# K and V laid out with 32 adjacent keys of one batch per partition (8 KB rows) in a fused attention and feed-forward gradient kernel

## Chip, cores, metric

One core of one Trainium2 chip. The metric is device time in microseconds (us); a quoted time is the median of a kernel's executions. Executions carry a state: "fast" or "slow" (over 1.5% above the fastest of the same kernel). All ratios below use fast executions alone. In the profile's lines PE is TensorE, PEld its weight loads, DVE VectorE, ACT ScalarE and POOL GpSimd.

## The reference, cut to what matters

The kernel computes the output and all eight gradients of one decode step: layer norm, then attention over the last 1024 keys of a cache (B = 4 batches, 8 key-value heads, 4 query heads for each, head size 128, one query), and beside it a gated feed-forward (512 to 1792).

```python
W = min(4096, max(256, Sk // 4))                  # 1024 of Sk = 4096 keys
k = jnp.repeat(k_cache[:, :, Sk - W:, :], rep, axis=1)
v = jnp.repeat(v_cache[:, :, Sk - W:, :], rep, axis=1)
scores = jnp.einsum("bhqd,bhkd->bhqk", q, k) * (Dh ** -0.5)
p = _softmax(scores, axis=-1)
o = jnp.einsum("bhqk,bhkd->bhqd", p, v)           # ... @ wo
# out = x + A(xn) + B(xn); then the gradients of x, K, V, wq, wo and the three B weights
```

Of the 112 MB that the kernel moves, 50 MB are zeros: the gradients of the 3072 keys of each head that the query does not see, written by DMA from one zero tile. K and V come in with 16.8 MB, and dK and dV of the 1024 keys in use go out with 16.8 MB.

## The kernel before, the parts that matter

The kernel runs four rounds of two key-value heads (`GP = 2`). In each it loads K and V, transposes them on TensorE for the scores, takes the softmax, transposes P (and dS) for the products o and dq, and makes dV and dK by outer products. Small pieces of output work lie in a list `bg` and are set in between other work by `tick`. The helper `evac` copies a result of TensorE out of its accumulation memory (PSUM), on VectorE or ScalarE. All DMA goes through three queues: loads from SyncE (q1), zeros from ScalarE (q10), stores from GpSimd (q0).

```python
outp = ctx.enter_context(tc.tile_pool(name="outp", bufs=3))      # buffers of output pieces (osb_*)
...
def load_kv(t, k, g):                   # partition m: 8 adjacent keys of each of 4 batches, 2 KB runs
    tl = kvpool[...].tile([P, B, J, Dh], BF16, name=nm, tag=nm)
    nc.sync.dma_start(out=tl[:].rearrange("p b j d -> p b (j d)"),
                  in_=src[:, t * GP + g, K0:Sk, :].rearrange("b (m j) d -> m b (j d)", j=J))
...
def scores(t, k):                       # for each head g and batch b
    for j in range(J):
        nc.tensor.transpose(T_ps[:, j, :], blks[(t, g)][:, b, j, :], ident[:])
    evac(T_sb[:], T_ps[:].rearrange("p j m -> p (j m)"), 1024, half=True)
    for q in range(NQ):                 # a quarter of the keys in each column tile
        nc.tensor.matmul(ps[q * RG:(q + 1) * RG, :], lhsT=lf[:, s * RG:(s + 1) * RG],
                         rhs=T_sb[:, q * WQ:(q + 1) * WQ], ..., tile_position=(0, q * RG))
    tick(2)
...
def by_quarter(src, nm):                # spread for dV and dK, on GpSimd
    nc.gpsimd.tensor_tensor(out=dst[:], in0=src[:]..., in1=qmsk[:]..., op=ALU.mult)

def transposed(src, nm):                # 2 transposes of P or dS itself, not of its spread
    for jj in range(JQ):
        nc.tensor.transpose(pT_ps[:, jj, :], src[:, jj * P:(jj + 1) * P], ident[:])
    evac(pT[:], pT_ps[:], 256, half=True)

def odq(t, k):                          # four batches in four column tiles, side by side
    for g in range(GP):
        for j in range(J):
            for b in range(B):
                nc.tensor.matmul(od_ps[b * RB:b * RB + rep, k, g, :], lhsT=pT[:, jj, c0:c0 + rep],
                                 rhs=blks[(t, g)][:, b, j, :], ..., tile_position=(0, b * RB))
...
# a round: masks, scores(K), softmax + dvdk(V), scores(V), softmax_d + dvdk(K), odq(o),
#          pre(t + 1), odq(dq), fin, load_next, dw
```

## Time and profile before

| before | |
|---|---|
| time, median of the first 3 executions | 289.91 us |
| span of the profiled execution | 287.5 us |
| DMA engines busy | 99.1% of the span: 284.9 us, idle 2.6 us |
| TensorE (PE) busy | 206.9 us |
| waits for stores of `osb_o`, in the chain | 17.92, 19.11 and 4.22 us |

The prediction shows the page's own lines. Three more lines of before are needed later. They are from the groups by shape; after the shapes come count, busy us, mean ns of one, then the idle us of the engine before them and what ended it:

```profile
L341 PE MATMUL S_ps<-T_sb,dom 128*32 128x256 bf16 x128 | 10.5, 310 | 5.1 <-DVE T_sb L94 5.1
...
L361 PE MATMUL pT_ps<-ident,P_b 128*128 128x128 bf16 x8 | 1.5, 283 | 3.5 <-ACT P_b L389 3.5
L361 PE MATMUL pT_ps<-ident,dS_b 128*128 128x128 bf16 x8 | 1.3, 244 | 4.9 <-DVE dS_b L405 4.9
```

The eight transposes of P and the eight of dS cost 2.8 us, and PE stands before them for 8.4 us, because P and dS come straight from ScalarE and VectorE. And from the waits (engine, tile, line, releaser; sum, count, longest), the two engines that fill the output buffers wait 37.0 us for a store to free one:

```profile
ACT osb_q L92 <- DMA out_dram<-osb_o: 20.1, 3, 9.5
...
DVE osb_q L94 <- DMA out_dram<-osb_o: 16.9, 3, 7.1
```

### The profile page before, as it was taken

The page shows a single profiled execution, that of the slowest core. Times are in us where ns is not written, and L with a number is a line of the kernel's source. Part 1 is how long each engine was busy: PE and PEld are TensorE (multiplying, and loading weights), DVE is VectorE, ACT ScalarE, POOL GpSimd, SP SyncE. Part 2 cuts the span into 40 slices and gives each one's busy share as a digit, 9 for nine tenths or more (in the row PEclk, how much of TensorE's full clock was granted, in tenths as well). Part 3 has the DMA queues.
Part 4 walks back from the last instruction along what each step waited for, and adds up shares of the span by engine and source line. Part 5 has one row for each costly group of instructions (what it writes and reads, how often), then busy time and mean ns, then how long its engine had stood idle before and what let it go on. Part 6 is the DMA issues. An engine that isn't in the chain of part 4 may idle for free.

```text
span 287.5 us, 6821 instructions
## 1 busy us (share of the span) xinstructions
PE 206.9 (72%) x2956; PEld 141.5 (49%) x2956; DVE 144.9 (50%) x310; ACT 113.7 (40%) x217; POOL 66.7 (23%) x84
## 2 busy tenths in 40 slices
PE   1397994983977999545689996546998679597710
PEld 0386882652644765333357654323665355364310
DVE  5484572333564567312626674126476525537770
ACT  1201653443442467312424563134355444336610
POOL 7000130441303152311033323110252132112410
PEclk9996899597897899795958898959799969959975
DMA  5999999999999999999998999999999999999897
GB/s 138 381 389 376 385 399 421 413 403 429 423 426 427 413 372 401 435 415 427 416 419 330 327 363 429 426 427 411 415 413 380 395 390 412 406 415 360 337 393 295
DMA packets 30182, 112.38 MB, mean 391 GB/s; under 512 B 1537, under 2 KB 7689, under 8 KB 26057
## 3 DMA queue, kind: packets, MB, share of 16 engines
q10 hardware_dynamic: 4612, 50.46, 41.9%
q1 hardware_dynamic: 17732, 30.81, 29.4%
q0 software_dynamic: 7808, 30.67, 27.3%
q8 instruction: 23, 0.38, 0.5%
q14 instruction: 7, 0.05, 0.0%
HBM read 30.93 MB, written 81.01 MB: 389 GB/s over the span
## 4 chain that ended last, share of the span: by engine, by line
PE 47%; DMA 28%; DVE 14%; issue 4%; ACT 2%; POOL 1%; SPq 0%; DVEq 0%; ACTq 0%; POOLq 0%
DMA out_dram<-osb_o 14%; PE T_ps L336 9%; PE kv_ps L444 7%; DMA out_dram<-stg_dv 4%; DVE T_sb L94 4%; PE S_ps L341 4%; DMA wd_sb<-in_B_w_down_dram 4%; DMA out_dram<-osb_d 3%; PE od_ps L416 3%; PE woT_ps L288 3%; PE wqT_ps L508 3%; DMA out_dram<-osb_g 2%; PE acc_ps L181 2%; PE wgT_ps L648 2%; PE wdT_ps L536 2%
## 5 line engine op out<-in xcount | busy, mean ns | idle before, releaser
L94 DVE COPY T_sb<-T_ps 128x1024 bf16<-128x1024 bf16 x64 | 44.2, 691 | 34.2 <-PE T_ps L336 33.7
L92 ACT CAST stg_dv<-kv_ps 128x512 bf16<-128x512 f32 x52 | 28.8, 589 | 43.2 <-PE kv_ps L444 42.8
L92 ACT CAST stg_dk<-kv_ps 128x512 bf16<-128x512 f32 x46 | 25.0, 588 | 15.4 <-PE kv_ps L444 13.1
L336 PE MATMUL T_ps<-ident,vb 128*128 128x128 bf16 x256 | 26.1, 251 | 6.6 <-DVE osb_q L94 6.6
L336 PEld LDWEIGHTS <-vb 128*128 128x128 bf16 x256 | 20.0, 114 | 12.7 <-issue 8.9
L92 ACT CAST osb_q<-dwq_ps 128x512 bf16<-128x512 f32 x25 | 13.6, 589 | 30.4 <-DMA out_dram<-osb_o 20.1
L336 PE MATMUL T_ps<-ident,kb 128*128 128x128 bf16 x256 | 24.4, 228 | 0.5 <-ACT stg_dk L92 0.3
L336 PEld LDWEIGHTS <-kb 128*128 128x128 bf16 x256 | 18.1, 101 | 12.4 <-issue 5.0
L444 PE MATMUL kv_ps<-domr,P_q 128*128 128x512 bf16 x64 | 23.9, 435 | 0.0
L444 PE MATMUL kv_ps<-qmr,dS_q 128*128 128x512 bf16 x64 | 20.9, 410 | 1.5 <-ACT stg_dk L92 1.0
L92 ACT CAST osb_g<-dwg_ps 128x384 bf16<-128x384 f32 (+1 forms) x30 | 14.5, 534 | 17.6 <-PE dwg_ps L621 8.1
L94 DVE COPY woT<-woT_ps 128x1024 bf16<-128x1024 bf16 x16 | 11.1, 692 | 17.2 <-PE woT_ps L288 17.2
L478 PE MATMUL dwq_ps<-od_r,xnm 128*128 128x256 bf16 x64 | 12.5, 320 | 6.8 <-DVE osb_q L94 6.6
L352 POOL TENSOR_TENSOR dS_q<-dS_b,qmsk 128x1024 bf16<-128x1024 bf16 x4 | 7.5, 1884 | 34.3 <-DVE dS_b L405 34.3
L92 ACT CAST osb_o<-dwo_ps 128x512 bf16<-128x512 f32 x23 | 12.7, 588 | 7.0 <-PE dwo_ps L463 6.8
L341 PE MATMUL S_ps<-T_sb,dom 128*32 128x256 bf16 x128 | 10.5, 310 | 5.1 <-DVE T_sb L94 5.1
L98 POOL DMA_DIRECT2D out_dram<-osb_q x8 | 5.8, 731 | 34.6 <-ACT osb_q L92 34.6
L94 DVE COPY wqT<-wqT_ps 128x1024 bf16<-128x1024 bf16 x16 | 11.0, 687 | 5.5 <-PE wqT_ps L508 5.3
L508 PEld LDWEIGHTS <-wq_sb 128*128 128x128 bf16 x128 | 11.1, 120 | 5.3 <-issue 4.3
L94 DVE CAST osb_q<-dwq_ps 128x512 bf16<-128x512 f32 x7 | 4.7, 689 | 16.9 <-DMA out_dram<-osb_o 16.9
L98 POOL DMA_DIRECT2D out_dram<-stg_dv x8 | 6.2, 774 | 30.4 <-ACT stg_dv L92 30.4
L94 DVE CAST stg_dk<-kv_ps 128x512 bf16<-128x512 f32 x18 | 12.0, 685 | 2.4 <-PE kv_ps L444 1.2
(187 smaller groups left out, 381.1 us busy)
## 6 DMA issues: line engine op xcount, KB each, us to landing
out_dram<-ztile ACTq DMA_DIRECT2D x8, 3072.0 KB, 16.5
out_dram<-ztile ACTq DMA_DIRECT2D x16, 1536.0 KB, 15.3
kb<-in_A_k_cache_dram SPq DMA_DIRECT2D x8, 1024.0 KB, 17.1
vb<-in_A_v_cache_dram SPq DMA_DIRECT2D x8, 1024.0 KB, 49.5
out_dram<-stg_dv POOLq DMA_DIRECT2D x8, 1024.0 KB, 10.1
out_dram<-stg_dk POOLq DMA_DIRECT2D x8, 1024.0 KB, 8.4
wo_sb<-in_A_wo_dram SPq DMA_DIRECT2D x4, 1024.0 KB, 10.2
wq_sb<-in_A_wq_dram SPq DMA_DIRECT2D x4, 1024.0 KB, 14.2
```

Source lines behind the costliest of these rows:

```text
L92: last.append(nc.scalar.copy(out=out, in_=in_))
L94: return nc.vector.tensor_copy(out=out, in_=in_)
L98: d = eng.dma_start(out=out, in_=in_)
L181: nc.tensor.matmul(ps[:, c, :], lhsT=lf(c), rhs=rhs, start=(k == 0), stop=(k == len(terms) - 1))
L288: nc.tensor.transpose(wT_ps[:, i, c, :], wo_sb[:, 2 * h2 + i, c * P:(c + 1) * P], ident[:])
L336: nc.tensor.transpose(T_ps[:, j, :], blks[(t, g)][:, b, j, :], ident[:])
L341: nc.tensor.matmul(ps[q * RG:(q + 1) * RG, :], lhsT=lf[:, s * RG:(s + 1) * RG], rhs=T_sb[:, q * WQ:(q + 1) * WQ], start=(g == 0 and b == 0 ...
L352: nc.gpsimd.tensor_tensor(out=dst[:], in0=src[:].unsqueeze(1).broadcast_to([P, NQ, WQ]), in1=qmsk[:].unsqueeze(2).broadcast_to([P, NQ, WQ] ...
L416: nc.tensor.matmul(od_ps[b * RB:b * RB + rep, k, g, :], lhsT=pT[:, jj, c0:c0 + rep], rhs=blks[(t, g)][:, b, j, :], start=(j == 0), stop=(j ...
L444: nc.tensor.matmul(mps[:].rearrange("p b d -> p (b d)"), lhsT=src[:, q, jj * P:(jj + 1) * P], rhs=mr[:, g].rearrange("p b d -> p (b d)"), ...
L478: nc.tensor.matmul(mps[:, i].rearrange("p g d -> p (g d)"), lhsT=xnm[:, i2 * 2 + i, c * P:(c + 1) * P], rhs=dq_r[:].rearrange("p g d -> p ...
L508: nc.tensor.transpose(wT_ps[:, i, c, :], wq_sb[:, c, h * Dh:(h + 1) * Dh], ident[:])
```

## The change

Intent: one partition holds 32 adjacent keys of one batch, so K and V come, and dK and dV go, in 8 KB runs instead of 2 and 4 KB, with fewer packets. The price is in the compute. A transposed block now has the four batches interleaved (key block and batch share the partition index), so the scores read T_sb with a step of 4. P and dS must be spread by batch *before* they are transposed. The o and dq products go over all four batches at once, in one column tile.

```diff
 def load_kv(t, k, g):
-    tl = ....tile([P, B, J, Dh], ...)          # J = 8
-    nc.sync.dma_start(out=tl[:].rearrange("p b j d -> p b (j d)"),
+    tl = ....tile([P, J, Dh], ...)             # J = 32; partition = (key block m, batch b)
+    nc.sync.dma_start(out=tl[:].rearrange("p j d -> p (j d)"),
 def scores(t, k):
-                    nc.tensor.matmul(ps[q * RG:(q + 1) * RG, :], lhsT=lf[:, s * RG:(s + 1) * RG],
-                                     rhs=T_sb[:, q * WQ:(q + 1) * WQ], ...
+                    nc.tensor.matmul(ps[b * RG:(b + 1) * RG, :], lhsT=lf[:, b, s * RG:(s + 1) * RG],
+                                     rhs=T_sb[:, :, b], ...
-    def by_quarter(src, nm):
+    def by_batch(src, nm):
+        nc.gpsimd.tensor_tensor(out=dst[:].rearrange("p j (m b) -> p (j m) b", b=B),
+                                in0=src[:].unsqueeze(2).broadcast_to([P, WQ, B]),
+                                in1=bmsk[:].unsqueeze(1).broadcast_to([P, WQ, B]), op=ALU.mult)
 def transposed(src, nm):                        # JQ = 8 transposes, was 2
-        evac(pT[:], pT_ps[:], 256, half=True)
+        evac(pT[:].rearrange("p j (h b) -> p j b h", b=B), pT_ps[:].rearrange("p j (b h) -> p j b h", b=B), 1024, ...)
 def softmax(t):
-        st[t].update(E=E_f, rr=rr, PT=transposed(P_b, "PT"), P=by_quarter(P_b, "P_q"))
+        P_x = by_batch(P_b, "P_x")
+        st[t].update(E=E_f, rr=rr, PT=transposed(P_x, "PT"), P=P_x)
 def odq(t, k):
-                for b in range(B):
-                    nc.tensor.matmul(od_ps[b * RB:b * RB + rep, k, g, :], lhsT=pT[:, jj, c0:c0 + rep],
-                                     rhs=blks[(t, g)][:, b, j, :], ..., tile_position=(0, b * RB))
+                nc.tensor.matmul(od_ps[0:rep * B, k, g, :], lhsT=pT[:, j % JQ, j // JQ, g], rhs=blks[(t, g)][:, j, :], ...)
 ...                                             # stores of dV and dK in 8 KB runs; masks; FFN rows: cut
```

> **What bounds the kernel now.** I read the page first, then the DMA view in short windows, the windows view by stage, the chain of waits, and last the groups by shape and the timeline. The page (busy time by engine, DMA share in 40 slices, DMA queues with packets, MB and share of 16 engines' span):
>
> ```profile
> PE 206.9 (72%) x2956; PEld 141.5 (49%) x2956; DVE 144.9 (50%) x310; ACT 113.7 (40%) x217; POOL 66.7 (23%) x84
> ...
> DMA  5999999999999999999998999999999999999897
> ...
> q10 hardware_dynamic: 4612, 50.46, 41.9%
> q1 hardware_dynamic: 17732, 30.81, 29.4%
> q0 software_dynamic: 7808, 30.67, 27.3%
> ```
>
> The DMA digits are 9 nearly everywhere, and the three queues add to 98.6% of the span (99.1% with instruction fetch): the DMA engines have no spare time. PE at 72% has some. So bytes per busy microsecond matter first. A queue's rate while busy is its MB over its share times 287.5 us: q10 (the zeros) 50.46/(0.419 x 287.5) = 419 GB/s, q0 (stores) 391 GB/s, q1 (loads) 364 GB/s. q1 mixes weights with K and V; from 24 to 32 us it carries K and V alone:
>
> ```profile
> q1 hardware_dynamic: 1535, 3.05, 103.4%
> ```
>
> That is 2 KB packets at 3.05/(1.034 x 8) = 369 GB/s. The stretch 206 to 214 us has all three queues at work:
>
> ```profile
> q10 hardware_dynamic: 197, 2.10, 62.4%
> q0 software_dynamic: 191, 0.78, 23.9%
> q1 hardware_dynamic: 205, 0.41, 13.3%
> ```
>
> About 200 packets each: the queues take turns packet by packet, so a queue's share follows its packet size (12 KB, 4 KB, 2 KB). Next, stages (stretch, its us, busy us of PE, PEld, DVE, ACT and POOL with counts, granted clock, DMA share, GB/s):
>
> ```profile
> 132.00:164.00 32.00, 27.76 (x429) 18.66 (x429) 16.25 (x36) 13.32 (x26) 8.63 (x7) 0.78 0.99 383
> ...
> 171.00:190.00 19.00, 9.64 (x129) 6.51 (x127) 5.63 (x13) 4.54 (x11) 3.87 (x4) 0.84 1.03 424
> 190.00:217.00 27.00, 22.65 (x363) 15.41 (x363) 15.37 (x34) 12.45 (x24) 8.07 (x7) 0.86 1.02 416
> ...
> 264.00:276.00 12.00, 7.10 (x38) 3.54 (x36) 7.98 (x13) 7.12 (x13) 3.76 (x5) 1.00 0.92 339
> 276.00:287.50 11.50, 0.30 (x3) 0.00 (x0) 3.90 (x9) 0.00 (x0) 0.72 (x1) 0.50 0.84 344
> ```
>
> PE is busy 27.8 of 32 us between 132 and 164 and 22.7 of 27 us between 190 and 217, but half idle from 171 to 190. The chain says why (start, us, what):
>
> ```profile
> 113.48 17.92 DMA out_dram<-osb_o
> ...
> 170.73 19.11 DMA out_dram<-osb_o
> ...
> 252.06 12.71 DMA out_dram<-stg_dv
> ```
>
> At the end of rounds 0 and 1 of the four rounds (t = 0..3), compute waits some 18 us for a store to free an output buffer. In between it is PE that paces, and only the work already queued keeps the DMA busy. Bytes issued minus bytes landed, in us at 400 GB/s, give that reserve: about 5 us at 104, 2.3 us at 160, 2.0 us at 216, 2.5 us at 236, under 1 us at 268. These low points are where added compute would leave the DMA idle.
>
> **What the Trainium skill says.** (1) "DMA: Bandwidth & Descriptors", Why small descriptors are slow: a fixed overhead of some cycles per packet, besides descriptor bytes. The trace agrees in direction: 369 GB/s at 2 KB, 419 at 12 KB. (2) "TensorE: Matmul & The Clock Gate", Part 3 (Packing small matmuls): matmuls at different column tiles run at once. The trace agrees, see od_ps below. (3) "Advanced Engine Details and Errata", VectorE Performance Modes: two elements a cycle from 16-bit data need a unit step innermost. The 1024-element copy in 691 ns fits two a cycle; no stepped copy stands in this trace. (4) The same page, Memory Cachelines: SBUF reads need two hits per 16-byte line for full speed; a step of 4 bf16 just has two. No run yet shows it.
>
> **The change, part by part.**
>
> DMA loads. 16 loads of 1.05 MB go from 2 KB to 8 KB packets. The trace's mean load packet takes 51 ns at 1 KB, 87 at 2 KB, 146 at 3.5 KB, so some 38 ns per further KB: estimate 323 ns at 8 KB, 406 GB/s. 16.8 MB take 45.5 us at 369 and 41.3 at 406: minus 4.2 us.
>
> DMA stores. 16 stores of 1.05 MB have 4 KB packets now (168 ns mean; two rows each); 7 KB packets take 273 ns and 12 KB ones 468, so 8 KB would take about 312 ns, 420 GB/s: minus 3 us. The means include crowded stretches (medians give half of it); I count 5.5 us for both, about 1.9%.
>
> Turns. K and V loads then move 8 KB a turn against 2, their stores 8 against 4, the zeros still 12. Zeros thus last longer as a reserve, and stg stores land sooner: worth about 1 us at each of the big waits.
>
> Compute, from the groups and the timeline:
>
> ```profile
> L94 DVE COPY T_sb<-T_ps 128x1024 bf16<-128x1024 bf16 x64 | 44.2, 691 | 34.2 <-PE T_ps L336 33.7
> ...
> L352 POOL TENSOR_TENSOR P_q<-P_b,qmsk 128x1024 bf16<-128x1024 bf16 x4 | 7.5, 1887 | 9.2 <-ACT P_b L389 9.2
> ...
> L416 PE MATMUL od_ps<-vb,PT 128*4 128x128 bf16 x256 | 7.0, 238 | 0.0
> ...
> L94 DVE COPY PT<-pT_ps 128x256 bf16<-128x256 bf16 x4 | 1.2, 292 | 4.3 <-PE pT_ps L361 4.3
> ```
>
> ```profile
> 216.35 0.61 PE L336 MATMUL T_ps<-ident,kb 128*128 128x128 bf16 x8
> ...
> 251.06 1.06 PE L416 MATMUL od_ps<-kb,dST 128*4 128x128 bf16 x64
> ```
>
> The o and dq products (od_ps): 64 matmuls took 1.06 us, less one drain of 0.22 about 13 ns each, because four batches sit in four column tiles. The 8 transposes, one after another in the whole array, took 56 ns each. After the change the four batches share one product over all 128 partitions: still 64 matmuls (32 key blocks, 2 heads), now in one tile. 64 x 56 = 3.6 us, plus 2.7 us a time, 8 times: plus 21 us of PE, more where the clock is low. This is the largest cost.
>
> P and dS. The spread on GpSimd (1.89 us, size unchanged) now stands before the transposes: 8 transposes for 2 (plus 6 x 0.056 = 0.34 us PE) and an evacuation of 1024 elements with a stepped output for 292 ns. At one element a cycle[...] that is about 1.2 us, plus 0.9 us DVE. The latency grows by 1.9 + 0.3 + 0.9 = 3.1 us, 8 times. For P it lies beside the V scores; for dS beside the next round's weight products, but in round 3 nothing is left to hide it.
>
> Unchanged: T_sb copies, kv_ps products and their evacuations (8 pieces per head before and after), masks, dw. Removed: 36 of 48 small matmuls in the FFN rows, some mask set-up, store descriptors on GpSimd. All early or off the path: about 0.
>
> **The sum.** Round 0: about 5 us more PE, reserve 5 us: 0 to 1 us of DMA idle. Round 1, from 132 to 160: what is left of the V product (42 of 64) +1.8, the K product +2.7, transposes and copy +0.5, about 5; PE gaps take 1, the reserve 2.3: 2 us idle. Round 2: +3.5 less 2.0, and a faster DMA empties its reserve sooner: 2 us. Round 3: two products +5.4, dS +3.1, less about 4 us of waits for stores in the last stretch and under 1 us of reserve: 4 us. Sum about plus 8.5; minus 5.5 for the DMA: plus 3. 289.9 + 3.1 = **293.0 us**.
>
> **Rivals.** (a) The compute is hidden and the DMA gain shows whole: 284 us. For it: 98.6% DMA share and 18 us waits; against it: the low reserves after those waits. (b) Compute takes over: PE, in order, stands at the transposes until GpSimd has spread P or dS, about 2 us eight times, besides the longer products: 298 to 304 us. Against it: the timeline shows od_ps and other work moved between the score steps, so other matmuls can be set in there. (c) The score products read with a step of 4: if that halved their rate, some 0.2 us for each of 64 groups, 10 us or more of PE: over 300. (d) Larger packets of loads delay osb_o stores (still 4 KB a turn) and lengthen the 18 us waits; their bytes are the same, so I give it 1 us at most.
>
> **Range and chances.** Low end: (a) at 284. High end: (b), 303. Faster by over 2% (under 284.1) needs nearly all the DMA gain and no idle: 0.13. Slower by over 2% (over 295.7) needs about 3 us more than my sum, easy for round 3 or the transposes: 0.35. Within: 0.52.
>
> **What would show it.** K/V loads alone at 400 GB/s or more in the DMA view, about 8 KB per packet; od_ps 64 at a time in 3.6 us; PT copies near 1.2 us; T_sb and S_ps unchanged; DMA digits below 9 near the ends of rounds and after 236 us. If the DMA share stays at 99%, the time must fall and I am wrong on idle; if pT_ps shows PE waits of 2 us, rival (b). What would make the prediction wrong: a schedule that fills PE better than I think, or a slower spread on GpSimd with inner runs of 4.

## The result

| | before | after |
|---|---|---|
| median | 290.73 us (4 executions) | 334.86 us (4) |
| range | 289.87 to 291.81 | 332.85 to 337.37 |
| ratio of fast executions | | 1.152, 95% interval 1.142 to 1.162 |

A ratio is the mean time of one kernel's fast executions over that of the other's of the same rounds, so it is not quite the ratio of the medians. The change made the kernel 15% slower.

The profile after, the page (busy by engine, DMA share in 40 slices, the three queues with packets, MB and share):

```profile
PE 241.3 (72%) x2968; PEld 170.5 (51%) x2968; DVE 160.8 (48%) x310; ACT 115.6 (34%) x219; POOL 62.8 (19%) x77
...
DMA  7999999996993399999916999999339959971895
...
q10 hardware_dynamic: 4624, 50.46, 35.8%
q1 hardware_dynamic: 11600, 30.81, 24.5%
q0 software_dynamic: 5760, 30.67, 23.2%
```

Read the DMA digits first. A solid row of 9s before; now holes, which the windows view places at about 100 to 120, 168 to 180, 236 to 252 and 296 to 316 us, with smaller ones at 80 and 272 us. The first large one (stretch, its us, busy us of PE, PEld, DVE, ACT and POOL with counts, granted clock, DMA share, GB/s) shows PE at work nearly throughout while the DMA engines are busy for 41% of it:

```profile
100.00:120.00 20.00, 18.49 (x256) 14.33 (x256) 10.33 (x19) 7.01 (x14) 4.68 (x4) 0.78 0.41 152
```

The queues add to 83.5%, 83.9% with instruction fetch. Of a span of 335.7 us that is 281.7 us busy and 54.0 idle, against 284.9 and 2.6 before. So the DMA did get shorter, by 3.2 us, and all of the loss is DMA idleness: compute had become the bound. What of compute? The groups by shape:

```profile
L418 PE MATMUL od_ps<-kb,dST 128*16 128x128 bf16 x256 | 19.6, 245 | 0.0
L418 PE MATMUL od_ps<-vb,PT 128*16 128x128 bf16 x256 | 16.6, 219 | 0.0
L341 PE MATMUL S_ps<-T_sb,dom 128*32 128x256 bf16 x128 | 12.9, 388 | 3.4 <-DVE T_sb L96 3.4
...
L96 DVE COPY PT<-pT_ps 128x1024 bf16<-128x1024 bf16 x4 | 9.7, 2432 | 14.9 <-PE pT_ps L363 14.9
L96 DVE COPY dST<-pT_ps 128x1024 bf16<-128x1024 bf16 x4 | 9.7, 2423 | 12.4 <-PE pT_ps L363 12.4
L352 POOL TENSOR_TENSOR P_x<-P_b,bmsk 128x1024 bf16<-128x1024 bf16 x4 | 7.6, 1889 | 11.3 <-ACT P_b L392 11.3
...
L363 PE MATMUL pT_ps<-ident,P_x 128*128 128x128 bf16 x32 | 4.1, 311 | 11.4 <-POOL P_x L352 11.4
L363 PE MATMUL pT_ps<-ident,dS_x 128*128 128x128 bf16 x32 | 3.9, 296 | 13.0 <-POOL dS_x L352 13.0
```

Four things stand here. The od products take 36.2 us of PE against 13.7. The stepped copies of PT and dST take 2.43 us each against 0.29, 19.4 us in all. PE stands 24.4 us before the transposes, waiting for GpSimd, against 8.4. And the score products take 388 ns instead of 310 (for the K half 386 instead of 287). The end of the chain of waits shows the first three in a row (start us, length us, what), in the last round:

```profile
290.72 1.89 POOL dS_x L352
292.66 1.05 PE pT_ps L363 x8
293.74 2.43 DVE dST L96
296.58 5.27 PE od_ps L418 x64
```

The same stretch before: 0.29 us for the two transposes, 0.29 for the copy and 1.06 us for 64 od products. The granted clock makes it worse. In the timeline the eight transposes take 1.03 us after 3.31 us in which PE was idle, where the prediction's line of before has eight in 0.61 us. In round 2, at a granted clock of 1.00, 54 products take 3.11 us (213.58 us), so 64 would take about 3.7; in this last round they take 5.27, and the granted clock is 0.50 from 289.6 to 299.8 us. The Trainium skill ("TensorE: Matmul & The Clock Gate", Part 1) says that the clock falls to half after an idle window of about 3.4 us. The trace agrees that the low clock stands at PE's pauses, but here no wholly idle window came first: in the 3.4 us before 289.6 us PE was busy for 2.26 us at a granted clock of 1.00.

The clock is no rival for the whole loss. Over a fast execution its mean was 0.814 to 0.822 in the changed kernel and 0.825 to 0.852 before, but the run a_tiled below, at 0.796 to 0.821, was 17.5 us faster than the changed kernel.

### The profile page after: what moved, and what is told of

Its sections match the earlier page's. It is cut to its first block, busy times and chain, and to the rows that moved or that the text cites. A ratio compares the mean times of both kernels' runs of the same rounds, so it can differ in the third digit from the quotient of the medians.

```text
span 335.7 us, 6838 instructions
## 1 busy us (share of the span) xinstructions
PE 241.3 (72%) x2968; PEld 170.5 (51%) x2968; DVE 160.8 (48%) x310; ACT 115.6 (34%) x219; POOL 62.8 (19%) x77
## 5 line engine op out<-in xcount | busy, mean ns | idle before, releaser
L94 ACT CAST stg_dk<-kv_ps 128x512 bf16<-128x512 f32 x46 | 25.5, 588 | 16.2 <-PE kv_ps L444 13.6
L444 PE MATMUL kv_ps<-domr,P_x 128*128 128x512 bf16 x64 | 22.5, 409 | 1.0 <-DVE od_T L429 1.0
L94 ACT CAST osb_g<-dwg_ps 128x512 bf16<-128x512 f32 (+1 forms) x30 | 14.8, 535 | 23.9 <-PE dwg_ps L620 13.1
L444 PE MATMUL kv_ps<-qmr,dS_x 128*128 128x512 bf16 x64 | 21.4, 411 | 0.6 <-ACT stg_dv L94 0.2
L418 PE MATMUL od_ps<-kb,dST 128*16 128x128 bf16 x256 | 19.6, 245 | 0.0
L418 PEld LDWEIGHTS <-dST 128*16 128x16 bf16 x256 | 17.4, 102 | 2.0 <-issue 1.9
L96 DVE COPY PT<-pT_ps 128x1024 bf16<-128x1024 bf16 x4 | 9.7, 2432 | 14.9 <-PE pT_ps L363 14.9
L418 PE MATMUL od_ps<-vb,PT 128*16 128x128 bf16 x256 | 16.6, 219 | 0.0
L96 DVE COPY dST<-pT_ps 128x1024 bf16<-128x1024 bf16 x4 | 9.7, 2423 | 12.4 <-PE pT_ps L363 12.4
L418 PEld LDWEIGHTS <-PT 128*16 128x16 bf16 x256 | 14.1, 90 | 2.8 <-issue 2.4
L352 POOL TENSOR_TENSOR dS_x<-dS_b,bmsk 128x1024 bf16<-128x1024 bf16 x4 | 7.5, 1884 | 38.7 <-DVE dS_b L409 38.7
```

The costliest lines, as they stand in the source:

```text
L94: last.append(nc.scalar.copy(out=out, in_=in_))
L96: return nc.vector.tensor_copy(out=out, in_=in_)
L352: nc.gpsimd.tensor_tensor(out=dst[:].rearrange("p j (m b) -> p (j m) b", b=B), in0=src[:].unsqueeze(2).broadcast_to([P, WQ, B]), in1=bmsk[ ...
L418: nc.tensor.matmul(od_ps[0:rep * B, k, g, :], lhsT=pT[:, j % JQ, j // JQ, g], rhs=blks[(t, g)][:, j, :], start=(j == 0), stop=(j == J - 1))
L444: nc.tensor.matmul(mps[:].rearrange("p q d -> p (q d)"), lhsT=src[:, jj, :], rhs=mr[:, g].rearrange("p q d -> p (q d)"), start=True, stop= ...
```

## Experiments

The theory after reading the traces: the DMA queue's reserve lasts only a few us, and once it is spent, every further us of PE time, copy time or spread latency lands in the total. Four suspects: the stepped copy, the untiled od product, the spread on GpSimd, and the place of the transposes in PE's program. Differences in us below are between medians; taken from the ratios times 290 us they come out up to 2 us larger or smaller. Rivals: the larger packets hurt in themselves; or one suspect is all of it and the rest is hidden in the 18 us waits for stores, where before had PE half idle; or the stepped score reads carry it.

### The DMA part alone: b_rows and b_rows2

The kernel before with 8 KB runs in loads and stores and nothing else. The result is wrong on purpose (loads and stores exchange keys and batches consistently, the sums in between do not).

```diff
-        nc.sync.dma_start(out=tl[:].rearrange("p b j d -> p b (j d)"),
-                      in_=src[...].rearrange("b (m j) d -> m b (j d)", j=J))
+        nc.sync.dma_start(out=tl[:].rearrange("p b j d -> p (b j d)"),
+                      in_=src[...].rearrange("b (m j) d -> m b (j d)", j=B * J))
 # and the same for the store from stg
```

> The kernel before with only the DMA part of the change: K and V loads and the dK/dV stores use 8 KB rows (one partition per key block and batch), everything else as before; its results are wrong on purpose, since compute still takes the rows for the old layout. Theory 'the DMA gain is real but small': loads near 403 GB/s and 8 KB store packets at 404 GB/s, as the changed kernel's packet records show, so 3 to 5 us of DMA time less and 285 to 288 us. Rival 'larger packets hurt by themselves' (turns between queues delay the buffers that compute waits for): 292 us or more.

Measured: 293.2 to 296.1 us in three fast executions, ratio 1.0113 (1.0025 to 1.0202). The profile fell in an odd execution of 540 us, in which matmuls were slow throughout (the K transposes 455 ns in the mean against 228); it is left out and its cause stays open. This is above the 285 to 288 us that I held likely and in the rival's range. I ran the same kernel again.

> The DMA part alone once more (same kernel as the first run, whose profile fell in an odd execution of 538 us with PE slow; its three timed runs were 293 to 296 us). Theory R (the reserve): the DMA time falls by about 3 us as in the changed kernel, but K and V loads, now 8 KB a turn, run out sooner, nothing is left beside compute at the ends of rounds, and the DMA idles there: queue shares sum to under 97% of the span, 292 to 296 us. Theory 'noise': 285 to 290 us with shares above 98%.

Measured: 293.59 us, ratio 1.0125 (1.0055 to 1.0195), in both cases slower than before. The 8 KB packets took 324 ns for loads and 326 for stores (404 and 402 GB/s over 16 engines), much as in the full change. The queue shares add to 95.9% of the span, under the 97% that the theory of the reserve named. The DMA part is thus not the cause of the 15%, but it is no gain either: it costs 1.2%. Where the 3 us come from is taken up below.

### The od product alone in the kernel before: b_serial

The batch loop moved outside, so that neighbouring matmuls are in the same column tile and do not overlap. Results stay right.

```diff
-            for j in range(J):
-                q, jj = j // JQ, j % JQ
-                for b in range(B):
+            for b in range(B):
+                for j in range(J):
+                    q, jj = j // JQ, j % JQ
```

> The kernel before with one edit: in the o and dq products the batch loop is outside the key loop, so that matmuls of one column tile follow one another and no longer run four at a time; same 64 matmuls, same result. 64 then take some 3.6 us against 1.06. Theory O (the product's lost packing is the main cause of plus 44 us): plus 15 us or more, 305 us up. Theory W (PE standing still at the transposes of P and dS behind the GpSimd spread and a long DVE copy is the main cause): plus 3 to 9 us, 293 to 299 us, since the added PE work fits partly into the waits for stores.

Measured: 294.24 us, ratio 1.0064 (0.9946 to 1.0183). The groups of b_serial:

```profile
L416 PE MATMUL od_ps<-vb,PT 128*4 128x128 bf16 x256 | 14.0, 242 | 0.0
L416 PE MATMUL od_ps<-kb,dST 128*4 128x128 bf16 x256 | 12.5, 250 | 0.0
```

12.8 us more PE work than before, and at most 1.8% of time, perhaps none. By itself, a product twice as long hides, in part in the waits for stores of `osb_o`, which fall from 37.0 to 32.3 us.

### The same product tiled again in the changed kernel: a_tiled

The 32 key blocks are split over four column tiles, and a small product with a 0/1 matrix adds the four parts when the rows are transposed.

```diff
-            for j in range(J):
-                nc.tensor.matmul(od_ps[0:rep * B, k, g, :], lhsT=pT[:, j % JQ, j // JQ, g], rhs=blks[(t, g)][:, j, :], ...)
+            for jj in range(JQ):
+                for q in range(NQ):
+                    nc.tensor.matmul(od_ps[q * RG:q * RG + rep * B, k, g, :], lhsT=pT[:, jj, q, g],
+                                     rhs=blks[(t, g)][:, q * JQ + jj, :], ..., tile_position=(0, q * RG))
-            nc.tensor.transpose(T_ps[:, g, :], rows[:, g, :], ident[:])
+            nc.tensor.matmul(T_ps[:, g, :], lhsT=rows[:, g, :], rhs=sel[:], start=True, stop=True)
```

> The changed kernel with the o and dq products spread over four column tiles again: each group of eight key blocks sums into its own 32 partitions, and the four partial sums are added by the next matmuls (a summing matrix in the transpose, masks that hold all four groups). 64 matmuls should take about 1.1 us again, 22 us of PE less in all. Theory N (once the DMA reserve is gone, every us of PE counts): minus 14 to 22 us, 313 to 321 us. Theory S (the stand at the transposes is what counts, the product hides in it, as it nearly did in the serial run of the kernel before: plus 3 us): minus 0 to 6 us, 329 to 335 us.

Measured: 317.34 us, ratio 1.0921 (1.083 to 1.1011), so 17.5 us less than the changed kernel. Its groups:

```profile
L423 PE MATMUL od_ps<-kb,dST 128*16 128x128 bf16 x256 | 7.8, 286 | 0.0
...
L423 PE MATMUL od_ps<-vb,PT 128*16 128x128 bf16 x256 | 5.8, 220 | 0.0
```

22.6 us of PE work gone (36.2 to 13.6), 17.5 us of time. The pair b_serial and a_tiled is the main lesson: **the same kind of work (12.8 us added there, 22.6 us removed here) is nearly free in a kernel with waits to hide it and is charged at about 0.8 us per us in one with few.**

### Unit-step copy: a_perm

The transposes go against a permuted identity, so the batches come out of TensorE in the order that the products want, and the copy is contiguous on both sides.

```diff
+    perm = const.tile([P, P], BF16, name="perm")
+    nc.vector.tensor_copy(out=perm[:].rearrange("p (h b) -> p b h", b=B), in_=ident[:].rearrange("p (b h) -> p b h", b=B))
-            nc.tensor.transpose(pT_ps[:, jj, :], src[:, jj, :], ident[:])
+            nc.tensor.transpose(pT_ps[:, jj, :], src[:, jj, :], perm[:])
-        evac(pT[:].rearrange("p j (h b) -> p j b h", b=B), pT_ps[:].rearrange("p j (b h) -> p j b h", b=B), 1024, half=True)
+        evac(pT[:], pT_ps[:], 1024, half=True)
```

> The changed kernel with the transposes of P and dS run against a permuted identity, so that their columns come out in the order wanted and the copy out of PSUM is a unit-step copy (expected 0.69 us, as the score copy of the same size) in place of the stepped one of 2.43 us. Eight copies, 1.74 us less each, 14 us of chain. Theory W: minus 9 to 15 us, 320 to 326 us. Theory O: minus 0 to 4 us.

Measured: 320.56 us, ratio 1.0969 (1.0875 to 1.1064), 14 us less than the changed kernel (16 us by the ratios). The group:

```profile
L96 DVE COPY PT<-pT_ps 128x1024 bf16<-128x1024 bf16 x4 | 2.8, 691 | 14.9 <-PE pT_ps L365 14.9
```

1.74 us less for each of eight copies are 13.9 us, and all of it shows in the time: the copies stand on the chain.

### Spread on VectorE: a_dve

One VectorE instruction takes the place of the scale on ScalarE or VectorE and the multiply on GpSimd.

```diff
-        nc.gpsimd.tensor_tensor(out=dst[:]..., in0=src[:]..., in1=bmsk[:]..., op=ALU.mult)
+        nc.vector.scalar_tensor_tensor(out=dst[:]..., in0=src[:]..., scalar=by[:, 0:1], in1=bmsk[:]...,
+                                       op0=ALU.mult, op1=ALU.mult)
```

> The changed kernel with P and dS spread by one VectorE instruction (scale times mask, about 1.1 us for 1024 elements) in place of a scale (0.51 us on ScalarE, 0.35 us on VectorE) and the GpSimd spread of 1.89 us: the leg before the transposes gets shorter by about 1.2 us, eight times. Theory S: minus 6 to 10 us, 325 to 329 us. If the spread on GpSimd is not what PE waits for: within 3 us of 335.

Measured: 323.52 us, ratio 1.109 (1.0951 to 1.1229), 11.3 us less than the changed kernel, a little more than I expected. The instruction took 1.28 us; PE's wait at the transposes fell from 24.4 to 15.0 us (6.6 and 8.4), so again about as much left the time as left the waits (9.4 us).

### The transposes later in PE's program: a_late

The transposes of P come two score steps later in the V scores, those of dS inside the next round's weight products, so that PE, which takes its program in order, has something else to do while GpSimd spreads.

```diff
 def scores(t, k):
+                if (k, g, q) == (1, 0, 2):
+                    st[t]["PT"] = transposed(st[t]["P"], "PT")
 def pre(t):
+            if t and h2 == 1:
+                st[t - 1]["dST"] = transposed(st[t - 1]["dS"], "dST")
```

> The changed kernel with the transposes of P set down in the program after two more score steps of V, and those of dS (rounds 0 to 2) inside the next round's weight products, so that PE has other work while GpSimd spreads; nothing else is changed. Theory W: PE waits for P_x and dS_x fall from 24 us to under 8 us and the time falls by 12 to 25 us, to 310 to 323 us. Theory O: within 4 us of 335, as the product is as long as before.

Measured: 328.49 us, ratio 1.1264 (1.1164 to 1.1364), 6.4 us less than the changed kernel: half of the smallest gain that I expected. PE's wait at the transposes did fall, from 24.4 to 7.7 us (4.4 and 3.3), but now ScalarE and VectorE waited for stores again (together 42.9 us for `osb_o`, against 12.5 in the changed kernel), and the 2.43 us copies and the long products stayed. So 16.7 us of PE's waiting gave 6.4 us of time: taking away one wait of several in a row uncovered the next.

### Together: a_all and a_all_late

a_all has the tiled product, the permuted identity and the VectorE spread; a_all_late also the late transposes.

> The changed kernel with three costs undone and the 8 KB rows kept: products in four column tiles, unit-step copies by a permuted identity, spread on VectorE. If the costs add as theory N has it: minus 14 (measured for the copy) minus 14 to 22 minus 6 to 10: 289 to 301 us. Under theory S: minus 20 to 30, 305 to 315 us.

Measured: 302.05 us, ratio 1.0409 (1.0324 to 1.0494), 32.8 us less than the changed kernel and 1 us above the range for costs that add. The three single gains add to 43.1; they overlap by 10 us, and waits for stores of `osb_o` come back (24.1 us on ScalarE and VectorE, against 12.5 in the changed kernel).

> As the run before it, with the transposes set down later in the program, so that PE has other work meanwhile. Setting them down later alone took 7 us off the changed kernel. Expected 3 to 6 us less than the run before it; if both theories are right about what is left (score products with a step of 4, 64 groups 0.11 us longer each by the trace, 7 us), 288 to 298 us; a version better than both kernels would be under 289.

Measured: 294.97 us, ratio 1.0127 (1.0013 to 1.024). The late transposes are worth 7.1 us here.

### The step of 4 in the score reads: b_step4 and a_s1

b_step4 is the kernel before with only the score products' moving operand read with a step of 4 (wrong result on purpose); a_s1 is a_all_late with K and V transposed against a permuted identity, so that the reads have unit step.

```diff
-                                     rhs=T_sb[:, q * WQ:(q + 1) * WQ], ...                                      # b_step4
+                                     rhs=T_sb[:].rearrange("p (n q) -> p n q", q=NQ)[:, :, q], ...
-                    nc.tensor.transpose(T_ps[:, jj, :], blks[(t, g)][:, q * JQ + jj, :], ident[:])             # a_s1
+                    nc.tensor.transpose(T_ps[:, jj, :], blks[(t, g)][:, q * JQ + jj, :], perm_m[:])
```

> The kernel before with the score products reading their moving operand with a step of 4 elements (wrong scores on purpose, same sizes). The trace of the changed kernel has four such matmuls in 0.40 us where the kernel before has 0.29. If the step is the cause: 0.40 us here too, 7 us of PE in 64 groups, 291 to 297 us since part of it hides in the waits for stores. If the cause is another one (the clock, other stationary operand): 0.29 us and within 1 us of before.

Measured: 291.74 us, ratio 1.0064 (0.9988 to 1.0139), unclear in time, but clear in the group: 389 and 386 ns, as in the changed kernel.

> The changed kernel with the three costs undone and the late transposes (295 us), and the K and V transposes run against a permuted identity that puts the keys of one batch side by side, so that the score products read with unit step. Four matmuls in 0.29 us again, 7 us of PE less: minus 3 to 6 us, 289 to 292 us, level with before. If the step does not matter: within 1.5 us of 295.

Measured: 293.47 us, ratio 1.0104 (1.0044 to 1.0163), 1.5 us above the range that I expected; the group is back at its old duration:

```profile
L351 PE MATMUL S_ps<-T_sb,dom 128*32 128x256 bf16 x128 | 10.5, 313 | 5.8 <-DVE T_sb L96 5.7
```

So the step costs some 5.5 us of PE time (25.6 against 20.1 us), and of the total at most a little: the ratios fall from 1.0127 to 1.0104, under 1 us and inside the scatter.

With this the compute part is undone: 293.5 us is what the DMA part alone gives (293.6). The agreement may be in part chance, since a_s1 also has two things that no version of the kernel before had in a run here, the spread on VectorE and the later transposes.

### Zeros moved: a_best

Four zero stores of each round moved from the V scores into the next round's weight products, to fill the small holes that a_s1 still has.

> As the run before it, with four of the twelve zero stores of a round issued late in the next round's weight products in place of the first V score steps, so that the DMA has work at the ends of rounds, where the trace shows empty queues at 104, 158 and 220 us. Theory R: minus 2 to 4 us, 285 to 289 us, better than before by up to 1.5%. If the holes merely move: within 1 us of the run before it.

Measured: 294.59 us, ratio 1.0141 (1.008 to 1.0201). No gain, where I had expected 285 to 289 us; the holes moved with the zeros.

### Why the DMA part alone costs time: b_ld and b_st

Loads alone, and stores alone, in 8 KB runs, in the kernel before (both wrong on purpose).

> The kernel before with the K and V loads alone in 8 KB rows (wrong result on purpose: the keys land in another order than the stores give back). Theory that the loads' larger turns delay the small output stores in the first 75 us: 293 to 296 us, ratio 1.009 to 1.018, as with both. Theory that the larger stores are the cause: 290 to 291.5, ratio under 1.004.

Measured: 307.5 us, ratio 1.0571 (1.0509 to 1.0633); the profiled execution (311.2 us) is of state slow, the five timed ones are fast. I expected the right direction, but a sixth to a third of the size and in another place (the first 75 us). The chain of waits of b_ld, where before had 17.92 and 19.11 us:

```profile
116.83 28.17 DMA out_dram<-osb_o
...
183.25 26.78 DMA out_dram<-osb_o
```

The two waits for a store to free an output buffer grew by 10.3 and 7.7 us, together 18.0, and the fast executions are 16 to 17 us slower than before. (The profile is of an execution counted slow; it is 3.7 us above the median, so it can carry the comparison of these waits only roughly.) My reading: the queues take turns by packet, and a load packet is now 8 KB where a store packet is 4, so the loads finish sooner and the stores that compute waits for later. The waits are measured; that turns cause them is argued. During the first wait itself the store queue is only a little slower (2.06 MB in the 24 us from 118 us on, 86 GB/s, against 1.48 MB in 16 us, 93 GB/s, before), so most of the longer wait probably comes from stores that were already behind when it began.

> The kernel before with the dK and dV stores alone in 8 KB rows (wrong result on purpose). Theory of the loads' turns: within 1 us of before, or up to 1.5 us faster, ratio 0.994 to 1.004. Theory of the stores as cause: 1.009 or more.

Measured: 294.1 us, ratio 1.0091 (1.0024 to 1.0159). My theory said under 1.004; this is a miss. Here the chain goes for 48.08 us, from 159.46 us on, through a load of K, where before it had none: with store packets of 8 KB and load packets of 2 KB the loads are what comes late. With both at 8 KB (b_rows2) the balance is about restored. Its two waits are nearly those of before:

```profile
116.68 18.89 DMA out_dram<-osb_o
...
174.68 19.27 DMA out_dram<-osb_o
```

That it is the relation of packet sizes and not one of the two sizes is what these three runs together show. Of b_rows2, 1.2% remain. In the two profiles the K transposes of round 0 start at the same time, 50.48 us; those of round 1 start at 108.16 us against 104.96, and the end comes 4.9 us later. So most of the loss is in round 0. The DMA engines are idle for 10.5 us against 2.6, and not in the first 75 us but at the ends of rounds (2.6 us of it from 156 to 160 us) and in the last stretch. In the first 75 us the waits for the stores of `osb_d` and `osb_g` took 9.64, 9.89 and 8.05 us in b_rows2's chain against 8.98 and 6.70 before; b_ld has them too (10.33, 9.99 and 7.95), b_st does not (10.24 and 7.20), so they come with the larger loads. Whether they make round 0 longer was not tested.

### A fourth output buffer: a_buf4m, with its controls b_buf4m, a_mr1 and after_buf4

If compute waits for output buffers, one more buffer should set the gain of the DMA free. Room comes from holding a round's masked rows once instead of twice (in the kernel before: the spread P and dS).

```diff
-    outp = ctx.enter_context(tc.tile_pool(name="outp", bufs=3))
+    outp = ctx.enter_context(tc.tile_pool(name="outp", bufs=4))
-            mr = attw.tile([P, GP, NQ, Dh], BF16, name=nm + "mr", tag=nm + "mr")
+            mr = attw.tile([P, GP, NQ, Dh], BF16, name=nm + "mr", tag=nm + "mr", bufs=1)
```

> The version with all compute repairs (293.5 us), with four output buffers instead of three; room is made by holding the masked rows of a round in one buffer instead of two. Theory that waits for output buffers keep the shorter DMA work from showing: 287 to 290 us, perhaps under the kernel before. Theory that compute sets the pace: within 1 us of 293.5, and the 18 us waits move or shrink with no gain. The single buffer of the masked rows can cost some of it.

Measured: 286.06 us, ratio 0.9844 (0.9783 to 0.9904), correct. It beats the kernel before by 1.6%, and is a little under my range. Its page:

```profile
DMA  6999999999999999999999999999998999997993
...
q10 hardware_dynamic: 4624, 50.46, 42.4%
q1 hardware_dynamic: 11600, 30.81, 28.1%
q0 software_dynamic: 5760, 30.67, 26.8%
```

The waits for stores of `osb_o` are gone from its list of waits (50.5 us in a_s1), and the row of 9s is back: 97.8% with instruction fetch of 284.3 us, 278 us of DMA work against 284.9 before.

> Control: the kernel before with four output buffers, room made by holding the spread P and dS in one buffer each. Its DMA work alone is 284.9 us, so no less than about 286. Theory of the buffers: 286 to 289. Theory of compute: 289 to 291, ratio 0.995 to 1.003.

Measured: 290.49 us, ratio 0.9979 (0.9925 to 1.0034). The kernel before gains nothing: its DMA was at 99% already. For the same reason the compute repairs, which were not run in the kernel before, could give it little.

> All compute repairs, three output buffers, masked rows of a round in one buffer instead of two: the control for the 286.1 us run. If the gain came from the fourth output buffer: 293 to 295 us, ratio 1.008 to 1.016, as the 293.5 us version, the waits for the store of osb_o still in the chain with 18 to 20 us. If it came from the single buffer: 285 to 288.

Measured: 296.45 us, ratio 1.0247 (1.019 to 1.0304): the single buffer of masked rows costs 1.4% against a_s1, a bit more than I allowed. The gain of a_buf4m is the fourth buffer's, and that is worth 0.9844 / 1.0247 = 0.961, about 4%. (The two runs are from different calls, each against its own runs of before.)

> The changed kernel as it stands with a fourth output buffer (room from the single buffer of masked rows). Theory that compute is its bound, as the undo runs say: 330 to 335 us, ratio 1.135 to 1.155, at most 4 us less than the changed kernel. Theory that waits for output buffers are a part of its loss: 322 to 328 us.

Measured: 327.54 us, ratio 1.1315 (1.1278 to 1.1352), 6 us (by the ratios) to 7 us (by the medians) less than the changed kernel. That is in the range of the theory that I held the less likely one: though its DMA idles for 54 us, a part of its loss is still waits for buffers (8.5 and 4.0 us on ScalarE and VectorE, which are gone here). Undoing compute remains the larger part.

## Why the prediction was wrong, point by point

| step, as the prediction put it | what the runs showed |
|---|---|
| packets at 8 KB about 323 and 312 ns | 326 and 324 ns: right (the 38 ns per KB that the text gives would make 317; 323 follows from its 2 and 3.5 KB packets) |
| od products 64 in 3.6 us, "the largest cost" | about 3.7 us at full granted clock, 5.27 us in the last round; plus 22.5 us of PE, forecast 21: right; undone, 17.5 us of time, where the sum let the reserve cover most of it |
| copy with a step "about 1.2 us" | 2.43 us; undone, 14 us |
| spread 1.89 us, "for P it lies beside the V scores; for dS beside the next round's weight products" | 1.89 us right, hidden wrong: PE stood 24.4 us; spread on VectorE 11.3 us, later transposes 6.4 us |
| "T_sb and S_ps unchanged" | T_sb yes; S_ps 310 to 388 ns, a group of four 0.11 us longer, half of what rival (c) named; undone, under 1 us |
| DMA "minus 5.5" | 3.2 us less busy in the changed kernel, 6.9 in a_buf4m, but alone plus 1.2% in time |
| rival (d) "I give it 1 us at most" | with loads and stores at 8 KB, as in the change (b_rows2), the two waits grew by 1.0 and 0.2 us: right; with loads alone at 8 KB, by 18.0 us and plus 5.7% |

**The step that failed** is the sum: how much longer a round becomes, and how much of that the DMA queue's reserve covers. For rounds 0 to 2 it added about 5, 5 and 3.5 us, nearly all of it PE work, and let the reserve (5, 2.3 and 2.0 us) and PE's gaps take most of it. The profiles show, for the stretch from a round's first K transpose to the next round's (round 3: to the end):

| | round 0 | round 1 | round 2 | round 3 |
|---|---|---|---|---|
| length before, us | 54.5 | 56.3 | 55.1 | 71.2 |
| length after, us | 73.3 | 64.9 | 65.7 | 84.7 |
| PE work added, us | 8.2 | 7.9 | 9.8 | 8.0 |
| DMA idle before, us | 0 | 0 | 0 | 3 |
| DMA idle forecast, us | 0 to 1 | 2 | 2 | 4 |
| DMA idle after, us | 15 | 10 | 10 | 19 |

The holes come to 54 us of idle in all against the 8.5 that I summed. Round 0 has them as much as the others, and no earlier hole can have used up its reserve. So it is not that one reserve was counted several times: the added time was far above the sum, and a cover of 2 to 5 us is small beside it. In rounds 1 and 2 the waits of 17.92 and 19.11 us that stood in the chain before are gone, which probably took up part of the added time; that was not tested. Undone one at a time, most costs came back nearly in full: 17.5 us for 22.6 us of PE in the products, 14 us for 13.9 us of copies, 11.3 us for the spread. The later transposes are the exception (6.4 us for 16.7 us of waiting).

The second failed step, and the larger part of what the sum left out, is the latency. I counted 3.1 us for each of P and dS, 25 us in all, and called most of it hidden, since other matmuls *could* be set in between. They were not: the transposes stand right behind the spread in PE's program, and PE stood idle before them for 24.4 us, against 8.4 before; the copies that follow took 19.4 us against 2.3. Rival (b) said exactly this, "PE, in order, stands at the transposes until GpSimd has spread P or dS", and its 298 to 304 us would have been nearer. I argued it away with the timeline of the kernel before, where od products and other work are set between score steps; but the transposes of P and dS were not among what is moved, and the groups by shape showed PE waiting for P_b and dS_b there already. Even (b) is 30 us short; it too took the copy at 1.2 us, and the runs with the spread and the copy undone (11.3 and 14 us) say that both stood in the chain.

The third: the copy was sized from a rule, one element a cycle, that no row of this trace showed. It was off by a factor of 2, eight times over (2.43 us for 1.2), and undoing the copies gave back 14 us.

The part of the mechanism that held: od products the largest cost, spread unchanged, packets as estimated, DMA digits below 9 near the ends of rounds. And the gain that the prediction sought is real: with all compute repairs and a fourth buffer, DMA work is 6.9 us less (278 against 284.9) and the time 4 us less than before.

What stays open: what makes round 0 of b_rows2 3.2 us longer, how the overlap of 10 us in a_all splits, and the 540 us execution.

## What to carry to other kernels

Slack that hides work is spent once. Before counting added work as hidden, add up all that a round puts on the chain, the waits and copies as well as PE's work, and set that against the slack; a test kernel that adds the work alone (b_serial) can look free while the full change is charged for it. An order of operands that TensorE sets nearly for nothing (a permuted identity: the transposes of P took 310 ns in the mean against 311, those of dS 309 against 296) beats a stepped copy after it. When one queue's packets grow, look at the transfers of the other queues that compute waits for, and give those more buffers before expecting the bandwidth to show.

## What the Trainium skill lacked or had wrong

- "Advanced Engine Details and Errata", VectorE Performance Modes and Memory Cachelines: the modes tell when a copy makes two elements a cycle, but not what a step costs. (Another page, "Vector Engine (DVE) Microarchitecture Reference", has measured costs of steps, but for 32-bit data.) A bf16 copy of 1024 elements out of PSUM with a step of 4 in its output took 2.43 us, against 0.69 us with unit step: 3.5 times as long, where the loss of the two-element mode alone would make it about twice. And two hits on each 16-byte line were not enough for full speed in TensorE's moving operand: with a step of 4 bf16 a score product of 256 columns took 389 ns in the mean against 310 (b_step4 and before), four side by side 0.40 us against 0.29.
- "DMA: Bandwidth & Descriptors", Queues, rings and completion order: it states that an engine goes round its queues packet by packet, and this case agrees (about 200 packets each in 8 us). It lacks what this can do to a kernel: larger loads alone made this one 5.7% slower, with waits for stores of 28.17 and 26.78 us instead of 17.92 and 19.11, while with stores made larger as well they were 18.89 and 19.27.
